# An attention and two-MoE kernel on one core: unused matmuls, the order of small transposes and differences in attention, and the place of a table load

## The chip, the cores and the metric

The kernel runs on one core of one Trainium2 chip. The metric is device microseconds (us) of one execution; lower is better. Three timed runs of the kernel before gave a median of 668.82 us (668.46 to 668.9). One further execution was profiled; all rows below are from it.

## The reference

Three stages in float32, each feeding the next:

```python
# attention: q, k, v are (2, 8, 576, 64); window 128; q and k are drawn 6.6 times larger than usual
scores = 0.125 * q @ k.T + bias                  # bias: -slope(head) * distance
scores = where((rel >= 0) & (rel < 128), scores, -1e9)
attn = exp(scores - max(scores)); attn = attn / (sum(attn) + 1e-9)
x = (attn @ v) reshaped to (1152, 512)
# MoE 1: four experts, w1 (4, 512, 1024), w2 (4, 1024, 512)
x = sum over e of p[:, e] * (relu(x @ w1[e]) @ w2[e])
# MoE 2: w_in (512, 2048), w_out (2048, 512), given as float64
h = x @ w_in
out = (h * cos(h)) @ w_out
```

## The kernel before, in words

Engines: TensorE (PE, its weight loads PEld), VectorE (DVE), ScalarE (ACT), GpSimd (POOL), and SyncE (SP), which issues the DMAs. The kernel switches the scheduler off, so each engine's queue holds its instructions in the order in which the loops write them.

**Attention** runs in 20 steps: two batches of five query blocks (the first of 64 rows, four of 128), each in two groups g = 0, 1 of four heads. `attention` (L494) is a software pipeline over k = 0 to 22. In round k, PE does the scores of step k (`att_scores`, L352, tile s_ps), the transposes of the probabilities of step k-2 (`att_transpose`, L419, tile t_ps; two halves m = 0 and m = 1) and the product with v of step k-3 (`att_pv`, L445, tile x_ps). DVE takes the row maxima of step k (L373), ACT the exponentials (L378); the half m = 0 of t_ps is copied out by DVE (L439), m = 1 by ACT (L441), both to tiles pt. There are two t_ps buffers, so a half of the next round can only be written when its copy of this round is done. For each query block (at g = 1) `att_sums` (L386, called one round after the scores) takes reciprocals of the row sums on DVE and spreads them on POOL (tile wide), and `att_factors` (L398, called two rounds after) transposes wide on PE (L405, tile r_ps), with a copy by ACT (L410, tile rs). `att_pv` then multiplies x_ps by rs on DVE (L469).

Between these calls stands `fill(k, s)`, s = 0, 1, 2 (L752), which spreads other work: for k < 9 at s = 0 two matmuls of the identity with itself whose result nobody reads (L757); the conversion of weights (`jobs`, on POOL); the first hidden layer of the first token block in halves (`plain`, L591, k = 12 to 19); three second-layer tiles (L666) at rounds 21 and 22; and `move`.

**The token blocks.** 1,152 tokens are three blocks of 384. The first goes through plain matmuls (operand xq). Blocks two and three go together through a product with seven multiplications in place of eight; its operands (tile xs) are made by `transform` (L282): three differences on DVE (t1, t2, b12; L299 to L301, shown at the helper's line L133), then seven roundings on ACT (L287) and seven remainders on DVE and POOL (L133), one `yield` after each. `transformed` (L327) runs the differences at once and leaves the rest in a list, from which `move(n)` (L335) takes n pieces. In attention it is called three times, in rounds 18, 20 and 22. The same function serves the turn from MoE 1 to MoE 2, there with a PSUM operand.

**The MoE groups** (`run`, L844) are 8 of MoE 1 and 4 of MoE 2, each a sequence of products (L569), plain matmuls (L597) and second layers (L666). Alongside, MoE 2's weights are converted from float64. In MoE 2 `cosine` (L533) evaluates cos as a Sin on ACT (L545); the activation table of that function is loaded by ACT_TABLE_LOAD, which in the kernel before stands directly ahead of the first such Sin.

Of the kernel before, what the change touches and what calls it, by code (L numbers as in the profile page):

```python
# [15 lines left out]
AF = mybir.ActivationFunctionType  # L16
# [18 lines left out]
NG1, NG2 = E * F1 // G, F2 // G  # L35
# [10 lines left out]
LAG = 2  # L46
# [3 lines left out]
def tile_kernel(ctx, tc, qT, kT, v, probs, w1, w2, w_in, w_out, out):  # L50
    nc = tc.nc
# [31 lines left out]
    def constants():  # L83
        rel_i, rel, msk = scr[:, 0].bitcast(I32), scr[:, 1], scr[:, 2]
        nc.gpsimd.iota(rel_i, pattern=[[-1, 256]], base=WIN, channel_multiplier=1)
        nc.vector.tensor_copy(rel, rel_i)
        nc.gpsimd.memset(msk, 0.0)
        big = -8.0e9
        nc.gpsimd.affine_select(
            out=msk, in_=msk, pattern=[[-1, 256]], compare_op=ALU.is_ge, fill=big,  # L90
            base=WIN, channel_multiplier=1,
        )
        nc.gpsimd.affine_select(
            out=msk, in_=msk, pattern=[[1, 256]], compare_op=ALU.is_ge, fill=big,
            base=-1, channel_multiplier=-1,
        )

        for h in range(H):
            slope = 2.0 ** (-8.0 * (h + 1) / H)
            nc.vector.scalar_tensor_tensor(  # L100
                out=bm[:, h, :], in0=rel, scalar=-8.0 * slope, in1=msk,
                op0=ALU.mult, op1=ALU.add,
            )
        make_identity(nc, ident)
# [18 lines left out]
    def load_values(b, i):  # L123
        s0, n = UNITS[i]
        vt = v_t[b, i] = qvp.tile([128, DM], F32, name="vt", tag="vt", bufs=5)
        nc.sync.dma_start(out=vt[:n], in_=v[b, s0 : s0 + n, :])
# [5 lines left out]
    def sub(eng, out, a, b):  # L132
        eng.tensor_tensor(out=out, in0=a, in1=b, op=ALU.subtract)  # L133
# [83 lines left out]
    def loads_ahead():  # L217

        if nload[0] < len(wq):
            raw_load(*wq[nload[0]])  # L220
            nload[0] += 1
# [60 lines left out]
    def transform(t, x1, x2, ps=None):  # L282

        def hi(k, src):
            nc.scalar.activation(out=xs[:, 0, k, :, ts], in_=src, func=AF.Copy)  # L287

        def lo(k, src, eng):
            sub(eng, xs[:, 1, k, :, ts], src, xs[:, 0, k, :, ts].bitcast(F32))  # L290

        ts = slice(t * 128, (t + 1) * 128)
        t1, t2 = (txp.tile([128, 2, 128], F32, name="tx", tag="tx") for _ in range(2))
        b11, b21, b12, b22 = x1[:, 0:2], x1[:, 2:4], x2[:, 0:2], x2[:, 2:4]
        if ps is None:
            ps = x2
        else:
            nc.scalar.activation(out=x2, in_=ps, func=AF.Copy)
        sub(nc.vector, t1, ps[:, 0:2], b11)  # L299
        sub(nc.vector, t2, ps[:, 2:4], t1)  # L300
        sub(nc.vector, b12, ps[:, 2:4], b12)  # L301
        yield

        hi(B11, b11)
        yield
        lo(B11, b11, nc.vector)
        hi(T2, t2)
        yield
        lo(T2, t2, nc.gpsimd)
        hi(T1, t1)  # L310
        yield
        lo(T1, t1, nc.vector)
        hi(T3, b12)
        yield
        lo(T3, b12, nc.gpsimd)
        hi(B21, b21)
        yield
        lo(B21, b21, nc.vector)
        sub(nc.vector, b21, b21, t2)
        hi(B22, b22)  # L320
        yield
        lo(B22, b22, nc.gpsimd)
        hi(T4, b21)
        yield
        lo(T4, b21, nc.vector)

    def transformed(*args):  # L327
        move(24)
        tr = transform(*args)
        next(tr)  # L330
        moved.append(tr)

    moved = []
# [1 line left out]
    def move(n):  # L335

        while moved and n:
            if next(moved[0], True):
                moved.pop(0)
            else:  # L340
                n -= 1
# [147 lines left out]
    def load_units_to(k):  # L489
        while nloaded[0] < min(k, len(units)):  # L490
            load_unit(*units[nloaded[0]])
            nloaded[0] += 1

    def attention(fill):  # L494
        at = lambda k, what: what(*steps[k]) if 0 <= k < len(steps) else None
        for k in range(len(steps) + LAG + 1):
            if k < len(steps) and k % 2 == 0:

                load_units_to(k // 2 + 3)
                load_values(*steps[k][0])  # L500
            at(k, att_scores)
            at(k - 1, att_sums)
            fill(k, 0)
            at(k - LAG, att_transpose)
            fill(k, 1)
            at(k - LAG - 1, att_pv)
            fill(k, 2)
            at(k - LAG, att_factors)


    pr = const.tile([128, NTT, E], F32, name="pr")
# [2 lines left out]
    def routing():  # L514
        nc.vector.tensor_reduce(out=prs, in_=pr, axis=mybir.AxisListType.X, op=ALU.add)
        nc.vector.tensor_scalar(out=prs, in0=prs, scalar1=1e-9, scalar2=None, op0=ALU.add)
        nc.vector.reciprocal(out=prs, in_=prs)
        nc.vector.tensor_tensor(
            out=pr, in0=pr, in1=prs.unsqueeze(2).to_broadcast([128, NTT, E]), op=ALU.mult
        )  # L520
# [6 lines left out]
    def advance():  # L527

        for ch in list(chains):
            if next(ch[1], True):  # L530
                chains.remove(ch)
# [59 lines left out]
    def plain(g, q, halves=False):  # L591

        w = operand(w_t[1, g, q // 2])
        ps = sums()[:, :NB]
        for d in range(ND):
            for a, bb in PASSES:
                nc.tensor.matmul(  # L597
                    ps, w(a, 2 * (q % 2) + d // 2, d % 2), xq[:, bb, d],
                    start=(d == 0 and (a, bb) == PASSES[0]),
                    stop=(d == ND - 1 and (a, bb) == PASSES[-1]),  # L600
                )
            if halves and d == 1:
                yield
        yield
        finish(g, ps, q, 0)
# [126 lines left out]
    def whole(step):  # L732
        for _ in step:
            pass

    with tc.manual_schedule():

        warm = ppool.tile([128, 4, 256], F32, name="warm", tag="p")
        nc.vector.memset(warm[:, 0], 0.0)
        nc.vector.memset(dens, 1e-9)  # L740
        for _ in range(WARM):
            nc.tensor.matmul(
                ps1.tile([128, 512], F32, name="o_ps", tag="o_ps")[:, :256],
                warm[:, 0, :128], warm[:, 0], start=True, stop=True,
            )
        load_units_to(2)
        constants()
        first = [None]

        turns = [(21, 1), (22, 1), (22, 2)]  # L750

        def fill(k, s):  # L752
            if s == 0 and k < 9:

                idle = ps1.tile([128, 512], F32, name="o_ps", tag="o_ps")
                for _ in range(2):
                    nc.tensor.matmul(idle[:, :128], ident, ident, start=True, stop=True)  # L757
            if (k, s) == (2, 0):
                for _ in range(RAWS):
                    loads_ahead()  # L760
            if (k, s) == (4, 0):
                nc.sync.dma_start(out=pr, in_=probs.rearrange("(t p) e -> p t e", p=128))
            if (k, s) == (11, 0):
                routing()
            if s == 0 and 4 <= k < 20:
                next(jobs)
            if s == 1 and 12 <= k < 20:
                q, half = divmod(k - 12, 2)
                if not half:
                    first[0] = plain(0, q, True)  # L770
                next(first[0])
            if s == 2 and 12 <= k < 20 and k % 2:
                whole(first[0])
            tile = None
            if (k, s) in turns:
                tile = layer2(0, turns.index((k, s)))
                next(tile)
            move(24 if (k, s) == turns[-1] else 2 * (s > 0))
            if tile:
                whole(tile)  # L780

        attention(fill)
    att.close()

# [59 lines left out]
    def run(groups):  # L844
        for g in groups:
            for step, stages, njobs, ncv in steps(g):
                next(step)
                move(2)
                for _ in range(stages):
                    advance()  # L850
                for _ in range(njobs):
                    next(jobs)
                for _ in range(ncv):
                    next(cv, None)
                next(step, None)
# [2 lines left out]
    cv = converts()  # L858
    with tc.manual_schedule():
        next(cv)  # L860
        run(range(NG1 - 1))
        left = sum(1 for _ in cv)
        assert not left, left
    cvs.close()
# [42 lines left out]
```

## Time and profile before

| | before |
|---|---|
| median of 3 runs | 668.82 us |
| the profiled execution | 669.17 us |
| its span, first to last instruction | 667.4 us |
| mean granted TensorE clock | 0.995 |
| PE busy | 654.1 us (98%) |
| DVE, ACT, POOL busy | 436.7, 331.5, 351.2 us |

The span is 1.77 us shorter than the time of the same execution, and that execution is 0.35 us above the median. Busy shares are averages over the span. A granted clock of 1.00 is TensorE at 2.4 GHz, 0.50 is 1.2 GHz.

### The profile page before, as it was taken

Reading aid. Unit: us, or ns where it says so; the run is one execution under the profiler, and the core shown is the slowest. Engines: PE = TensorE matmul, PEld = TensorE weight load, DVE = VectorE, ACT = ScalarE, POOL = GpSimd, SP = SyncE. Lnnn points to the kernel's source line nnn. Section 1 sums busy time; section 2 is a strip of 40 time slices with the busy share of each in tenths; the row PEclk is TensorE's granted clock in tenths of the full one; section 3 lists DMA queues with packets and bytes.
Section 4 is the critical chain, followed back from the end, with each engine's and each line's share of the span. In section 5 each row is a group of like instructions: output and inputs, shape, how many; then the busy total and the mean of one; then the engine's idle time right before and its main releaser. Section 6 shows DMA issues by size and latency. Waiting matters only on the chain.

```text
span 667.4 us, 9861 instructions
## 1 busy us (share of the span) xinstructions
PE 654.1 (98%) x3604; PEld 577.8 (87%) x3604; DVE 436.7 (65%) x830; ACT 331.5 (50%) x759; POOL 351.2 (53%) x342
## 2 busy tenths in 40 slices
PE   9999899999999999999999999999899999999998
PEld 7787689898998998998998988987798988988976
DVE  6675877868767768679678572546674563673662
ACT  6786635444343444353253341346673673673660
POOL 2664528447256265275174192284547747757740
PEclk9999899999999999999999999999899999999999
DMA  8362111624515426326326231120000200200102
GB/s 243 84 192 70 32 32 50 220 79 159 174 54 164 149 78 204 110 80 215 118 64 220 79 96 32 31 95 1 24 8 33 94 1 32 94 1 31 49 32 94
DMA packets 39872, 60.42 MB, mean 91 GB/s; under 512 B 5648, under 2 KB 22288, under 8 KB 39824
## 3 DMA queue, kind: packets, MB, share of 16 engines
q1 hardware_dynamic: 39824, 59.80, 28.2%
q8 instruction: 28, 0.46, 0.3%
q14 instruction: 20, 0.16, 0.1%
HBM read 49.04 MB, written 10.75 MB: 90 GB/s over the span
## 4 chain that ended last, share of the span: by engine, by line
PE 83%; DVE 8%; ACT 6%; issue 2%; POOL 1%; DVEq 0%; ACTq 0%; POOLq 0%
PE o_ps L666 38%; PE o_ps L569 21%; PE o_ps L597 13%; PE x_ps L457 3%; PE s_ps L362 3%; PE t_ps L429 2%; DVE u L541 2%; ACT r L539 2%; ACT u L538 2%; POOL hpair L133 1%; DVE u L547 1%; PE o_ps L757 1%; DVE c L612 1%; DVE xs L133 1%; DVE o_ps L612 1%
## 5 line engine op out<-in xcount | busy, mean ns | idle before, releaser
L666 PE MATMUL o_ps<-w2t,hpair 128*128 128x512 f32 x852 | 204.2, 392 | 1.6 <-POOL hpair L133 1.4
L666 PEld LDWEIGHTS o_ps<-w2t,hpair 128*128 128x128 f32 x852 | 158.6, 188 | 34.5 <-POOL hpair L133 2.7
L569 PE MATMUL o_ps<-xs,w1t 128*128 128x384 f32 x1008 | 183.0, 338 | 4.0 <-DVE c L612 3.1
L569 PEld LDWEIGHTS o_ps<-xs,w1t 128*128 128x128 f32 x1008 | 176.6, 189 | 8.5 <-DVE c L612 4.4
L597 PE MATMUL o_ps<-xq,w1t 128*128 128x384 f32 x576 | 110.4, 338 | 0.0
L133 POOL TENSOR_TENSOR w1t<-raw,w1t 128x512 fp32r<-128x512 f32 x48 | 65.1, 1367 | 84.3 <-ACT w1t L156 80.6
L133 POOL TENSOR_TENSOR w2t<-raw,w2t 128x512 fp32r<-128x512 f32 x48 | 67.3, 1419 | 70.9 <-ACT w2t L156 70.6
L597 PEld LDWEIGHTS o_ps<-xq,w1t 128*128 128x128 f32 x576 | 101.6, 188 | 3.3
L666 PE MATMUL o_ps<-w2t,h 128*128 128x512 f32 x432 | 103.7, 393 | 0.0
L666 PEld LDWEIGHTS o_ps<-w2t,h 128*128 128x128 f32 x432 | 81.0, 189 | 16.2 <-issue 0.2
L133 POOL TENSOR_TENSOR w1t<-sm,w1t 128x512 fp32r<-128x512 f32 x48 | 63.6, 1335 | 45.7 <-ACT w1t L156 45.4
L541 DVE SCALAR_TENSOR_TENSOR u<-r,u 128x384 f32<-128x384 f32 x48 | 39.9, 840 | 62.1 <-ACT r L539 58.5
L133 POOL TENSOR_TENSOR hpair<-u,hpair 128x384 fp32r<-128x384 f32 x32 | 33.0, 1054 | 39.5 <-ACT hpair L549 39.5
L156 ACT ACTIVATE w1t<-sm 128x512 fp32r<-128x512 f32 x44 | 27.5, 626 | 35.3 <-POOL sm L133 35.3
L378 ACT ACTIVATE p<-p,nmax 128x256 f32<-128x256 f32 (+2 forms) x80 | 36.2, 454 | 16.0 <-DVE nmax L373 15.8
L254 ACT ACTIVATE cr<-cr 128x512 f32<-128x512 f32 x32 | 21.6, 676 | 44.8 <-DVE cv L248 44.8
L681 DVE SCALAR_TENSOR_TENSOR accpair<-o_ps,pr,accpair 128x512 f32<-128x512 f32 x42 | 31.3, 745 | 17.8 <-PE o_ps L666 17.8
L556 ACT ACTIVATE hpair<-o_ps 128x384 fp32r<-128x384 f32 x48 | 23.4, 488 | 36.5 <-DVE o_ps L612 35.9
L242 ACT ACTIVATE cr<-cr 128x512 int32<-128x512 uint32 x32 | 21.6, 677 | 39.0 <-DMA cr<-w_in 27.0
L557 DVE SCALAR_TENSOR_TENSOR hpair<-o_ps,hpair 128x384 fp32r<-128x384 f32 x48 | 26.6, 554 | 20.3 <-ACT hpair L556 20.3
L248 DVE SCALAR_TENSOR_TENSOR cv<-cr,cv 128x512 int32<-128x512 int32 x32 | 34.1, 1066 | 1.1
L545 ACT ACTIVATE u<-u 128x384 f32<-128x384 f32 x48 | 24.7, 518 | 20.3 <-DVE u L541 20.3
(111 smaller groups left out, 833.7 us busy)
## 6 DMA issues: line engine op xcount, KB each, us to landing
raw<-w SPq DMA_DIRECT2D x32, 512.0 KB, 3.9
cr<-w_in SPq DMA_DIRECT2D x16, 512.0 KB, 4.4
cr<-w_out SPq DMA_DIRECT2D x16, 512.0 KB, 4.5
wi<-cv SPq DMA_DIRECT2D x16, 256.0 KB, 3.8
wo<-cv SPq DMA_DIRECT2D x16, 256.0 KB, 2.2
raw<-wi SPq DMA_DIRECT2D x8, 512.0 KB, 3.3
raw<-wo SPq DMA_DIRECT2D x8, 512.0 KB, 3.5
qt<-qT SPq DMA_DIRECT2D x8, 256.0 KB, 2.9
```

The source lines that it names most:

```text
L133: eng.tensor_tensor(out=out, in0=a, in1=b, op=ALU.subtract)
L156: nc.scalar.activation(out=out, in_=src, func=AF.Copy)
L248: nc.vector.scalar_tensor_tensor(out=a, in0=hw, scalar=-0x40000000, in1=o, op0=ALU.bitwise_and, op1=ALU.bitwise_or,)
L378: nc.scalar.activation(out=p[:n, k, :wid], in_=p[:n, k, :wid], func=AF.Exp, scale=-1.0, bias=nmax[:n, k : k + 1], accum_out=den[:n, k, 0:1],)
L541: nc.vector.scalar_tensor_tensor(out=u, in0=r, scalar=MAGIC, in1=u, op0=ALU.subtract, op1=ALU.subtract)
L545: nc.scalar.activation(out=u, in_=u, func=AF.Sin, scale=-TWOPI)
L556: nc.scalar.activation(out=hi, in_=src, func=AF.Relu)
L557: nc.vector.scalar_tensor_tensor(out=lo, in0=src, scalar=0.0, in1=hi.bitcast(F32), op0=ALU.max, op1=ALU.subtract)
L569: nc.tensor.matmul(ps, w(a, k, m), xs[:, bb, b, m], start=(start and m == 0 and (a, bb) == PASSES[0]), stop=(stop and m == 1 and (a, bb) = ...
L597: nc.tensor.matmul(ps, w(a, 2 * (q % 2) + d // 2, d % 2), xq[:, bb, d], start=(d == 0 and (a, bb) == PASSES[0]), stop=(d == ND - 1 and (a, ...
L666: nc.tensor.matmul(ps, h0[:, a, f, t * 128 : (t + 1) * 128] if t < NQ else hpair[:, a, f, (t - NQ) * 128 : (t - NQ + 1) * 128], w_t[2, g, ...
L681: nc.vector.scalar_tensor_tensor(out=o, in0=ps, scalar=s, in1=o, op0=ALU.mult, op1=ALU.add)
```

## The change

Four edits:

1. The two unused matmuls stand in rounds 0 to 3 only, no longer in rounds 4 to 8.
2. `att_factors` moves from the end of a round to directly behind `att_transpose`.
3. A `transform` that is called from attention starts with two empty pieces and is no longer advanced at once; `move` takes three pieces at s = 1, in place of two. So the differences of a block come one round later, behind that round's row maxima.
4. The table of Sin is loaded by an instruction of its own after group 0 of MoE 1.

```diff
@@ transform
         if ps is None:
+            yield
+            yield
             ps = x2
@@ transformed
         tr = transform(*args)
-        next(tr)
+        if len(args) > 3:
+            next(tr)
         moved.append(tr)
@@ attention
             fill(k, 0)
             at(k - LAG, att_transpose)
+            at(k - LAG, att_factors)
             fill(k, 1)
             at(k - LAG - 1, att_pv)
             fill(k, 2)
-            at(k - LAG, att_factors)
@@ fill
-            if s == 0 and k < 9:
+            if s == 0 and k < 4:
@@ fill
-            move(24 if (k, s) == turns[-1] else 2 * (s > 0))
+            move(24 if (k, s) == turns[-1] else (0, 3, 2)[s])
@@ the first MoE loop
         next(cv)
-        run(range(NG1 - 1))
+        run(range(1))
+        nc.scalar.preload_act_table(AF.Sin)
+        run(range(1, NG1 - 1))
```

PE in round 5, before: scores, the unused pair (o_ps from ident), transposes of the probabilities, product with v, transposes of wide.

```order
L362 MATMUL s_ps<-xk,qt 128x256 x4
L757 MATMUL o_ps<-ident 128x128 x2
L429 MATMUL t_ps<-ident,p 64x128 x2
L429 MATMUL t_ps<-ident,p 128x128 x2
L429 MATMUL t_ps<-ident,p 64x128 x2
L429 MATMUL t_ps<-ident,p 128x128 x2
L457 MATMUL x_ps<-pt,vt 64x128 x8
L405 MATMUL r_ps<-ident,wide 128x128 x4
```

The same round 5 after the change:

```order
L365 MATMUL s_ps<-xk,qt 128x256 x4
L432 MATMUL t_ps<-ident,p 64x128 x2
L432 MATMUL t_ps<-ident,p 128x128 x2
L432 MATMUL t_ps<-ident,p 64x128 x2
L432 MATMUL t_ps<-ident,p 128x128 x2
L408 MATMUL r_ps<-ident,wide 128x128 x4
L460 MATMUL x_ps<-pt,vt 64x128 x8
```

The unused pair is gone, and the four transposes of wide stand ahead of the product with v.

DVE at the end of round 18 and in round 19, the last with scores, before (L373's rows, ISA, are the row maxima; four pairs of them stand there; the tx and xk rows of L133 are the differences; xs is the first remainder):

```order
L439 COPY pt<-t_ps 128x512
L469 TENSOR_TENSOR xk<-x_ps,rs 128x512
L133 TENSOR_TENSOR tx<-xk 128x256
L133 TENSOR_TENSOR tx<-xk,tx 128x256
L133 TENSOR_TENSOR xk<-xk 128x256
L133 TENSOR_TENSOR xs<-xk,xs 128x2x128
L373 ISA p,nmax<-s_ps,bm 128x256
L373 ISA nmax 128x1
```

After the change, from the last pair of the row maxima on:

```order
L376 ISA p,nmax<-s_ps,bm 128x256
L376 ISA nmax 128x1
L442 COPY pt<-t_ps 128x512
L133 TENSOR_TENSOR tx<-xk 128x256
L133 TENSOR_TENSOR tx<-xk,tx 128x256
L133 TENSOR_TENSOR xk<-xk 128x256
L133 TENSOR_TENSOR xs<-xk,xs 128x2x128
L560 SCALAR_TENSOR_TENSOR h_128<-o_ps,h_128 128x384
L133 TENSOR_TENSOR xs<-tx,xs 128x2x128
L394 TENSOR_REDUCE rec<-dens 128x8
L397 RECIPROCAL rec<-rec 128x8
L442 COPY pt<-t_ps 128x512
```

The row maxima of step 19 and the copy of t_ps behind them now stand ahead of the differences; the copy of the next round stands behind the differences, three remainders and the reciprocal.

ACT at the turn to MoE 2, before (f_ps is a transposed output tile, u the argument of the cosine):

```order
L298 ACTIVATE accpair<-f_ps 128x512
L287 ACTIVATE xs<-accpair 128x2x128
L287 ACTIVATE xs<-tx 128x2x128
L545 ACT_TABLE_LOAD
L545 ACTIVATE u<-u 128x384
L156 ACTIVATE w1t<-sm 128x512
```

ACT where group 0 ends, after the change:

```order
L254 ACTIVATE cr<-cr 128x512
L559 ACTIVATE h_128<-o_ps 128x384
L865 ACT_TABLE_LOAD
L621 ACTIVATE p_1718<-o_ps 128x384
L156 ACTIVATE w2t<-raw 128x512 x2
```

The load has moved from the turn to the end of group 0; each program has two loads in all, the other being the one of Exp at the start.

## Rows read from the trace of the kernel before

**Rows 1.** The page, busy time by engine, and the granted clock in 40 slices.

```profile
PE 654.1 (98%) x3604; PEld 577.8 (87%) x3604; DVE 436.7 (65%) x830; ACT 331.5 (50%) x759; POOL 351.2 (53%) x342
...
PEclk9999899999999999999999999999899999999999
```

**Rows 2.** The chain of waits, 12 to 29 us: start, length, engine, tile, line.

```profile
12.79 0.64 PE o_ps L757 x4
...
14.68 1.06 PE s_ps L362 x8
...
28.62 0.64 PE o_ps L757 x4
```

**Rows 3.** The timelines of DVE and ACT: start, length, instruction; copies of t_ps in round 4.

```profile
14.53 0.70 DVE L439 COPY pt<-t_ps 64x256 f32<-64x256 f32 x2
...
15.34 0.63 ACT L441 ACTIVATE pt<-t_ps 64x256 f32<-64x256 f32 x2
```

**Rows 4.** Windows: length, then busy us of PE, PEld, DVE, ACT, POOL; clock, DMA, GB/s.

```profile
11.60:31.10 19.50, 19.50 (x186) 14.71 (x185) 12.20 (x55) 15.66 (x56) 11.04 (x13) 1.00 0.55 157
31.10:40.20 9.10, 9.10 (x106) 7.27 (x104) 6.92 (x36) 8.32 (x33) 7.84 (x11) 1.00 0.60 171
```

**Rows 5.** The second of these windows, the transposes of L429 alone: PE, PEld.

```profile
31.10:40.20 9.10, 3.28 (x24) 2.57 (x24) 1.00 0.60 171
```

**Rows 6.** The timeline of PE in rounds 19 and 20; in brackets idle time and releaser.

```profile
68.73 1.14 PE L362 MATMUL s_ps<-kt,qt 64*128 64x256 f32 x8
...
72.89 0.66 PE L405 MATMUL r_ps<-ident,wide 128*128 128x128 f32 x4
75.53 0.66 PE L429 MATMUL t_ps<-ident,p 128*128 128x128 f32 x4 [1.98 <-DVE pt L439]
```

**Rows 7.** The chain of waits, 60 to 92 us.

```profile
69.64 0.82 DVE tx L133
...
73.50 0.33 DVE p L373
...
75.95 0.48 ACT pt L441
...
78.03 0.48 ACT rs L410
...
79.05 1.95 PE t_ps L429 x8
```

**Rows 8.** The timeline of DVE, the first difference of the next block.

```profile
80.77 0.43 DVE L133 TENSOR_TENSOR tx<-xk 128x256 f32<-128x256 f32 x1
```

**Rows 9.** Windows around the two slices with a lower clock.

```profile
75.00:80.00 5.00, 3.87 (x29) 3.07 (x30) 3.38 (x9) 4.61 (x14) 1.49 (x3) 0.74 0.13 49
80.00:85.00 5.00, 5.00 (x36) 4.04 (x35) 4.50 (x10) 2.13 (x6) 2.89 (x4) 0.92 0.01 3
460.00:465.00 5.00, 4.04 (x21) 3.09 (x20) 4.32 (x8) 2.63 (x6) 1.82 (x3) 1.00 0.02 3
480.00:485.00 5.00, 5.00 (x19) 4.65 (x18) 2.70 (x6) 3.69 (x8) 2.65 (x3) 0.66 0.35 107
```

**Rows 10.** The chain of waits at the turn to MoE 2.

```profile
453.33 1.28 ACT L545
...
454.62 0.53 ACT u L545
...
479.48 3.65 PE o_ps L569 x12
```

**Rows 11.** The timeline of DVE there: the operation on whose result the first Sin works.

```profile
453.44 0.55 DVE L541 SCALAR_TENSOR_TENSOR u<-r,u 128x384 f32<-128x384 f32 x1
```

**Rows 12.** PE's waits from 450 to 490 us: total, times, longest.

```profile
PE o_ps L569 <- DVE c L612: 2.1, 1, 2.1
PE f_ps L714 <- DVE accpair L681: 1.0, 1, 1.0
```

**Rows 13.** The timeline of ACT at the end of group 0.

```profile
132.66 0.49 ACT L618 ACTIVATE p<-o_ps 128x384 f32<-128x384 f32 x1 [1.11 <-PE o_ps L569]
```

## The prediction

> **What bounds the kernel now.** I read the page first. PE is busy 98% of the span [rows 1], so a gain must take work from PE, fill one of its few idle stretches, or raise its clock. The line of the granted clock shows two of 40 slices below 9: the fifth, 67 to 83 us, the end of attention, and the 29th, 467 to 484 us, the turn to MoE 2 [rows 1, 9]. The chain of waits then says who sets the pace. From 5 to 68 us it is PE without a break, with the unused pairs in it (five of them from 12 to 29 us [rows 2]). From 69 to 79 us it leaves PE for DVE and ACT [rows 7], and again up to 479.5 us at the turn, with the table load as one link [rows 10]. Apart from the first microsecond PE waits nowhere else for longer than 0.7 us. All four edits touch these places.
>
> **Edit 1, the unused pairs.** Rounds 4 to 8 each lose 0.64 us of PE on the chain: 5 x 0.64 = 3.2 us [rows 2]. Between 11.6 and 31.1 us PE is never idle [rows 4], so these are real time, unless what PE would meet 0.64 us earlier isn't ready. ACT is the next limit: it works 15.66 us in that window, PE would need 19.5 - 3.2 = 16.3, so ACT is close behind but not ahead [rows 4]. Round by round I find one wait. In round 5 the scores would end at 15.1 (12.79, plus 1.25 for the transposes and the product with v of round 4, plus 1.06 for the scores). The transposes behind them need both copies of t_ps of round 4. DVE's ends at 14.53 + 0.70 = 15.2, ACT's at 15.34 + 0.63 = 16.0 [rows 2, 3]. The second half, due near 15.6, waits about 0.4 us. Later rounds have their copies 0.5 us or more before the need, because there ACT's work moves up along with the scores. What is saved is 3.2 - 0.4 = **2.8 us**. The bounds are 3.2 (no wait) and 0 (ACT takes over in every round). I stay near the first, since rounds 9 to 11 run without pairs already and PE does not idle there, with ACT busy 8.32 of 9.10 us [rows 4].
>
> What else could the pairs be for? The clock. In rounds 9 to 11 there is no pair and no hidden layer, transposes of t_ps fill 3.28 of the 9.10 us, and the clock is 1.00 throughout [rows 4, 5]. So I price the loss of the pairs' cover at nothing. The Trainium skill speaks against this edit: in "TensorE: Matmul & The Clock Gate", Part 4, it says that the clock's upper level does not engage for transposes, which do not count as PE activity in the same way. By that rule the rounds without pairs could fall to the lower level; that is a rival below, priced from rows.
>
> **Edit 2, the factors' transposes.** The same four matmuls, 0.66 us [rows 6], come about 1 to 2 us earlier in the round. They need wide, which POOL finishes in the round before, so PE does not wait. ACT then finds r_ps ready right behind its copy of t_ps. PE is the bound in these rounds, so by itself this is **0**; it only helps edit 3. Its cost bound is a wait for wide, a few tenths.
>
> **Edit 3, the differences.** Before, step 15's product ends and DVE starts on the differences at 69.64; the row maxima of the last scores, ready at 68.73 + 1.14 = 69.87, start only at 73.50 [rows 6, 7]. Everything behind them is late by 3.6 us: DVE's copy of t_ps, for which PE waits 1.98 us [rows 6], then ACT's exponentials and copies, for which it waits twice more for 0.3. And the clock: 0.74 over 75 to 80 us and 0.92 over 80 to 85 means (0.26 x 5 + 0.08 x 5) x 2 = 3.4 us at 1.2 GHz [rows 9], in which work takes twice as long. That costs 1.7 us; the eight transposes at 79.05 take 1.95 in it [rows 7], 1.0 at the upper level. As one sum: PE ends the factors' transposes at 73.5 [rows 6] and starts the last block of transposes at 79.05, 5.6 us for transposes and a product that take about 1.0 each at the upper level: 3.6 lost. With 0.9 more for the slow transposes, 4.5 us are lost.
>
> After: the row maxima start at 69.9. From their start to ACT's copy of t_ps it is 75.95 - 73.50 = 2.45 us [rows 7], so the copy runs from 72.35 to 72.8. DVE's copy, right behind the row maxima (four at 0.35), ends near 71.9. PE comes to the transposes of round 20 at 73.5, as before [rows 6], and finds both: **the wait of 1.98 is gone**. PE then does transposes and product until 75.6. Late next is the copy of round 20 on DVE, now behind more work. From 72.35 ACT does its copy (0.48 [rows 7]), rs (as much), two roundings, the hidden layer's rounding and a third rounding, an estimated 2.3 us, to 74.7; DVE then that rounding's remainder (0.4, as the operation of [rows 8]), the reciprocal (an estimated 0.3) and the copy (0.7 [rows 3]), to 76.1 or, with a pause or two, 76.4. So PE waits 0.5 to 0.9 us; I take 0.9. The differences themselves cost less there: 0.43 each when POOL is quiet, against 0.82 [rows 7, 8]. A wait of this size leaves the clock up: from 460 to 465 us PE is idle for 0.96 and the clock stays 1.00 [rows 9, 12]. So the edit saves 4.5 - 0.9 = **3.6 us**. Bounds: 4.5 (no wait left) and 0 (the wait comes back whole one round later). The last block's differences were the last thing before the products of MoE 1; one remainder now stands ahead of them on DVE, 0.4 us, where PE had about as much to spare, so nothing for that.
>
> **Edit 4, the table load.** It takes 1.28 us at 453.33; the first Sin starts at 454.62 [rows 10]. Its argument is ready at 453.44 + 0.55 = 453.99 [rows 11]. Without the load Sin could start at 454.0, so **0.6 us** leave a chain that runs through DVE and ACT from there to 479.48 without PE [rows 10]. PE collects them in its wait of 1.0 us on the accumulator, which shrinks to 0.4 [rows 12]; the wait of 2.1 behind it stays, since both sides move. Bounds 0 and 1.28. At its new place the load fills ACT's pause of 1.11 us [rows 13] and makes ACT 0.2 late; the product's copy is needed by a second pass of PE more than 2 us on. Cost 0. No table load is added after it, since all that ACT does from there on (copy, relu, abs, Sin) stands behind one load in the built order.
>
> **Sum.** 2.8 + 0 + 3.6 + 0.6 = 7.0 us. Against the profiled execution, 669.17, that is 662.2; that execution lies 0.35 above the median, so I predict **661.8 us**. Between 92 and 450 us PE waits for nothing, so what is gained in attention is handed on. A measurement of this kernel can tell some 0.2%, 1.3 us, from no change.
>
> **Rivals.**
> - *The wait moves.* PE finds round 20's copy on DVE later than I reckon, idles some 2 us and the clock falls as before; edit 3 then gives about 1.0 in place of 3.6: 664.4. For it: eleven DVE operations with waits on ACT stand ahead of that copy. Against: each is priced from rows, and POOL is quieter by then.
> - *ACT takes over.* The pairs were hidden; edit 1 gives 0.3 in place of 2.8: 664.3. For it: ACT at 15.66 of 16.3. Against: rounds 9 to 11 [rows 4].
> - *Better: the second slow stretch goes too.* At 480 to 485 the clock is 0.66, again 3.4 us at 1.2 GHz and 1.7 us lost, after PE's wait of 2.1 [rows 9, 12]. That wait now falls at another moment of the run. If the clock then stays up: 661.8 - 1.7 = 660.1.
> - *Slower: the clock falls in attention.* Without pairs, rounds 4 to 8 run at 1.2 GHz. Their 16.3 us of PE work [rows 4] take 16.3 more: 678.1. It decides once about 14 us are spent at the lower level, since each costs half and the gain is 7.0. For it stands only the skill's sentence above; against it, the clock of 1.00 in rounds 9 to 11 [rows 4, 5].
> - *No change.* The edits don't do what they say. The built order shows that they do; what is left is that the wait moves and ACT takes over at once, and the load was hidden: within 0.2%, 668.
>
> **Chances.** Forecast 0.52; the wait moves 0.20; ACT takes over 0.09; better 0.12; slower 0.04; no change 0.03. The first four are faster: 0.93. The range goes from the better case to just beyond the two weaker gains, 659.7 to 664.9; it leaves out the last two cases and some of the mixed ones (wait moved and pairs hidden, 666.9).
>
> **What would show it.** Right: the slice at the end of attention has clock 9; no wait of PE on L439's copy of about 2 us, but one under 1 us at the last block of transposes; the scores of round 9 start 2.8 us earlier; the first product of MoE 1 starts 6.4 us earlier; PE's wait on the accumulator at the turn is near 0.4. Wrong: a wait of PE in each of rounds 4 to 8; a slow slice between 12 and 40 us; a PE wait of 2 us or more in rounds 20 or 21; a pause of PE near 131 us; or a third ACT_TABLE_LOAD.

## The result, and the profile after

The changed kernel takes **661.44 us** (median of 5 executions, 661.05 to 661.97), the kernel before, on the same chip, 668.82 (668.32 to 669.02, 5 executions). The ratio is 0.9892, with a 95% interval of 0.9877 to 0.9906: faster by 1.1%. The prediction was 661.8 with a range of 659.7 to 664.9. The execution that was profiled took 661.97, its span is 660.2 and its mean granted clock 0.999. Line numbers are 2 or 3 higher than before: L362 is now L365, L429 is L432, L405 is L408, L439 and L441 are L442 and L444, L569 is L572.

The page after, busy time by engine and the granted clock, beside [rows 1]:

```profile
PE 649.2 (98%) x3584; PEld 573.0 (87%) x3584; DVE 435.2 (66%) x830; ACT 330.7 (50%) x759; POOL 350.8 (53%) x342
...
PEclk9999999999999999999999999999999999999999
```

PE has 20 matmuls fewer, the five pairs (each matmul of a pair is two instructions here), and 4.9 us less of busy time. Both slices with a lower clock are gone.

The waits of PE over the whole span: total, times, longest.

```profile
PE o_ps L572 <- DVE c L615: 3.0, 4, 2.1
...
PE o_ps L572 <- ACT p L621: 1.1, 3, 0.6
...
PE f_ps L717 <- DVE accpair L684: 0.3, 1, 0.3
```

No line on pt is left, where before PE waited 1.98 us on DVE's copy [rows 6]. The wait on the accumulator fell from 1.0 to 0.3, and the one on c is as long as it was [rows 12]. New is 0.6 us on ACT, at 482.51.

The chain of waits in rounds 4 to 9:

```profile
12.36 1.11 PE s_ps L365 x8
...
16.06 0.54 ACT pt L444 x2
...
16.64 0.63 PE t_ps L432 x4
17.27 0.44 PE r_ps L408 x4
...
22.73 1.06 PE s_ps L365 x8
23.80 1.02 PE t_ps L432 x8
...
29.39 1.06 PE s_ps L365 x8
```

The same chain before, with a pair up to round 8 and none from round 9 on:

```profile
11.81 0.98 PE s_ps L362 x8
...
25.07 0.87 PE t_ps L429 x8
...
31.16 1.06 PE s_ps L362 x8
32.23 1.02 PE t_ps L429 x8
```

The transposes now come directly behind the scores. From the scores of round 4 to those of round 9 it is 29.39 - 12.36 = 17.03 us, against 31.16 - 11.81 = 19.35 before: 2.32 less. Only once in these rounds does the chain leave PE, between the scores of round 4 and the transposes of round 5, for the exponentials of round 4 and ACT's copy behind them (16.06). Without a wait the transposes of round 5 would end at 16.88 (its scores end at 15.86, plus 1.02); they end at 17.27, so 0.4 us are lost. Two things were not forecast: eight transposes take 1.02 us here where they took 0.87 behind a pair, and the factors' transposes take 0.44 where they took 0.59. Round 4 itself starts 0.55 later than in the profile of before. That is start-up: the first pair takes 1.15 us here and 0.73 there, the scores behind it 0.59 and 0.38, together 0.63, and the factors' transposes of round 3 give 0.08 back. Up to there the two kernels have the same order on PE but for these; the first pair takes 0.64 to 1.15 us in the profiles of this case.

The timeline of PE in rounds 19 to 21:

```profile
67.44 1.09 PE L432 MATMUL t_ps<-ident,p 128*128 128x128 f32 x8
...
70.98 1.09 PE L432 MATMUL t_ps<-ident,p 128*128 128x128 f32 x8
...
73.19 1.36 PE L432 MATMUL t_ps<-ident,p 128*128 128x128 f32 x8
```

The timeline of DVE there, the last row maximum and what now stands behind it:

```profile
68.58 0.42 DVE L376 CUSTOM_DVE_ANT_0 p<-s_ps,bm 128x256 f32<-128x256 f32 x1
...
68.92 0.69 DVE L442 COPY pt<-t_ps 128x512 f32<-128x512 f32 x1
69.53 0.50 DVE L133 TENSOR_TENSOR tx<-xk 128x256 f32<-128x256 f32 x1
```

The end of the chain in attention:

```profile
66.44 1.11 PE s_ps L365 x8
67.56 0.41 DVE p L376
...
73.28 0.57 DVE pt L442
...
73.89 0.66 PE t_ps L432 x4
74.54 0.44 PE r_ps L408 x4
...
85.66 9.40 PE o_ps L572 x53
```

The same before; at 68.83 the product ends and the scores of round 19 begin:

```profile
67.78 1.05 PE x_ps L457 x16
...
92.09 14.59 PE o_ps L569 x84
```

The transposes of round 20 (70.98) follow without a break. At the last block (73.19) PE idles 0.17 us before the first half and a little between the halves, 0.5 in all (the product ends at 72.00 + 1.02 = 73.02 and the transposes would end at 74.04; they end at 74.54). From the scores of round 19 to the first product of MoE 1 it is 85.66 - 66.44 = 19.22 us, before 92.09 - 68.83 = 23.26: 4.04 less.

So the first product of MoE 1 starts 6.43 us earlier (92.09 to 85.66): 2.32 from rounds 4 to 8, 0.62 from rounds 9 to 18, 4.04 from the end of attention, less 0.55 of start-up. In that product 0.18 is lost again (its 84 matmuls take 14.77 us, 14.59 before; a weight load waits 0.2 for DVE's c).

The timeline of ACT at the new place of the load:

```profile
125.32 1.28 ACT L865 ACT_TABLE_LOAD   x1
126.62 0.49 ACT L621 ACTIVATE p<-o_ps 128x384 f32<-128x384 f32 x1
```

At the turn PE comes to the accumulator 6.25 us earlier than before and leaves it 6.86 earlier (462.59 to 455.73): the load is worth 0.61.

The product behind the wait on c, in the timeline of PE, where before it took 3.65 us [rows 10]:

```profile
472.62 2.35 PE L572 MATMUL o_ps<-xs,w1t 128*128 128x384 f32 x12 [2.06 <-DVE c L615]
```

### The profile page after: what moved, and what is told of

Same layout as the page of the kernel before. It is cut to its first block, busy times and chain, and to the rows that moved or that the text cites. A ratio compares the mean times of both kernels' runs of the same rounds, so it can differ in the third digit from the quotient of the medians.

```text
span 660.2 us, 9818 instructions
## 1 busy us (share of the span) xinstructions
PE 649.2 (98%) x3584; PEld 573.0 (87%) x3584; DVE 435.2 (66%) x830; ACT 330.7 (50%) x759; POOL 350.8 (53%) x342
## 4 chain that ended last, share of the span: by engine, by line
PE 83%; DVE 7%; ACT 6%; issue 2%; POOL 1%; ACTq 0%; DVEq 0%; POOLq 0%
PE o_ps L669 38%; PE o_ps L572 21%; PE o_ps L600 14%; PE s_ps L365 3%; PE x_ps L460 3%; DVE u L544 2%; PE t_ps L432 2%; ACT r L542 2%; ACT u L541 2%; POOL hpair L133 1%; DVE u L550 1%; DVE c L615 1%; DVE xs L133 1%; DVE o_ps L615 1%; ACT p L381 1%
## 5 line engine op out<-in xcount | busy, mean ns | idle before, releaser
L572 PE MATMUL o_ps<-xs,w1t 128*128 128x384 f32 x1008 | 182.5, 336 | 4.8 <-DVE c L615 3.0
L572 PEld LDWEIGHTS o_ps<-xs,w1t 128*128 128x128 f32 x1008 | 175.5, 188 | 10.2 <-DVE c L615 4.8
L133 POOL TENSOR_TENSOR w1t<-raw,w1t 128x512 fp32r<-128x512 f32 x48 | 65.0, 1364 | 84.3 <-ACT w1t L156 80.7
L133 POOL TENSOR_TENSOR w2t<-raw,w2t 128x512 fp32r<-128x512 f32 x48 | 67.2, 1418 | 71.2 <-ACT w2t L156 70.9
L133 POOL TENSOR_TENSOR w1t<-sm,w1t 128x512 fp32r<-128x512 f32 x48 | 63.4, 1330 | 45.0 <-ACT w1t L156 44.7
L133 POOL TENSOR_TENSOR hpair<-u,hpair 128x384 fp32r<-128x384 f32 x32 | 32.6, 1039 | 39.5 <-ACT hpair L552 39.5
```

The costliest lines, as they stand in the source:

```text
L572: nc.tensor.matmul(ps, w(a, k, m), xs[:, bb, b, m], start=(start and m == 0 and (a, bb) == PASSES[0]), stop=(stop and m == 1 and (a, bb) = ...
```

## The experiments

Eleven kernels in twelve runs: each edit alone, two edits left out of the whole, and variants of the pairs and of the two orders. Each expectation stands as it was written before the run. "Before" is the kernel before on the same chip. The interval of a ratio, in brackets, is some 0.9 us to either side (0.6 for edits 2 and 4 alone), so times alone tell two variants apart only from about 1.3 us on; smaller differences between variants rest on the traces.

**Edit 1 alone** (the kernel before with this):

```diff
-            if s == 0 and k < 9:
+            if s == 0 and k < 4:
```

> Edit 1 alone: the unused pairs in rounds 0 to 3 only. Theory P (the prediction's term): 5 x 0.64 = 3.2 us less 0.4 of one wait, 2.8 us gained, near 666.0. Theory S (from the two traces): the transposes behind the scores take 1.02 us on the chain, behind a pair 0.87, so a pair costs PE only 0.49 net; 5 x 0.49 = 2.4, less 0.5 of waiting in round 5: 1.9 gained, near 666.9. Rival (the pairs hold the clock up): a granted clock of 0.5 somewhere between 12 and 40 us, and no gain or a loss.

666.45 us (665.81 to 667.48, 5 executions), before 668.78; ratio 0.9968 (0.9956 to 0.9981): 2.3 us. The chain of waits of its profile, rounds 4 to 9:

```profile
12.40 1.04 PE s_ps L362 x8
...
18.70 0.59 PE r_ps L405 x4
...
23.91 1.02 PE t_ps L429 x8
...
29.66 1.06 PE s_ps L362 x8
```

29.66 - 12.40 = 17.26, so 2.09 less than before. The time lies between the two theories, 2.8 and 1.9, and its interval (1.3 to 2.9 us) holds both; the trace decides for Theory S. The transposes take 1.02 here too, so the 0.15 us that they lose belong to the missing pair, while r_ps keeps its 0.59.

**Edit 2 alone:**

```diff
             at(k - LAG, att_transpose)
+            at(k - LAG, att_factors)
...
-            at(k - LAG, att_factors)
```

> Edit 2 alone: the factors' transposes directly behind the probabilities' ones. Theory P: 0, PE does the same work, 668.8. Theory S: behind transposes of the same shape the four take 0.44 us on the chain in place of 0.59 behind the product with v, in eight rounds with 128 rows and two with 64 (0.08 less): 8 x 0.15 + 2 x 0.08 = 1.4 at most, less the one or two rounds in which PE waits anyway; near 667.6.

667.79 us (667.38 to 669.18, 11 executions), ratio 0.9986 (0.9977 to 0.9995): 1.0 us where I had 0. The profile of this run is also the test of the clock's share, since its granted clock is 9 in every slice of its page and 1.00 in the mean. Its timeline of PE at the end of attention:

```profile
74.61 0.66 PE L429 MATMUL t_ps<-ident,p 128*128 128x128 f32 x4 [2.14 <-DVE pt L439]
...
78.12 0.66 PE L429 MATMUL t_ps<-ident,p 128*128 128x128 f32 x4 [0.88 <-ACT pt L441]
79.28 0.66 PE L429 MATMUL t_ps<-ident,p 128*128 128x128 f32 x4 [0.51 <-DVE pt L439]
```

Its first difference, in the timeline of DVE:

```profile
68.64 0.88 DVE L133 TENSOR_TENSOR tx<-xk 128x256 f32<-128x256 f32 x1
```

Its window over the same stretch as in [rows 9]:

```profile
75.00:80.00 5.00, 3.32 (x34) 2.44 (x33) 3.36 (x9) 3.79 (x11) 1.93 (x3) 1.00 0.00 0
```

At the upper level the last block's transposes still start at 78.12 and 79.28, because they wait for ACT and DVE (0.88 and 0.51). From the first difference (68.64 here, 69.64 before [rows 7]) to the end of these transposes it is 11.30 us here (79.28 + 0.66) and 11.36 before (79.05 + 1.95). The slow stretch cost no time: it filled a wait. The executions of the kernel before say the same. Of 21 in this comparison, 12 have a mean granted clock of 0.995, with a median of 668.70, and 7 have 1.00, with 668.85.

**Edit 3 alone:**

```diff
         if ps is None:
+            yield
+            yield
...
-        next(tr)
+        if len(args) > 3:
+            next(tr)
...
-            move(24 if (k, s) == turns[-1] else 2 * (s > 0))
+            move(24 if (k, s) == turns[-1] else (0, 3, 2)[s])
```

> Edit 3 alone: the differences behind the next round's row maxima. Theory P: 3.6 us gained, 665.2; PE's wait of 2 us on the copy of t_ps gone, the slow stretch at the end of attention gone. Rival (the gain needs edit 2, because ACT's copy of r_ps then comes late in the round and the remainders behind it): a wait of over 1 us stays at the last block of transposes, the gain is 2.5 or less.

665.09 us (664.74 to 665.24, 5 executions), ratio 0.9945 (0.9931 to 0.9958): 3.7 us, as forecast. The list of PE's waits has none on a copy of t_ps any more (at the last block 0.17 us are left on the chain, behind ACT's copy). The first product of MoE 1 starts at 87.60, against 92.09; rounds 4 to 9 take 19.35, as before. From the scores of round 19 to that product it is 87.60 - 68.47 = 19.13 us, against 23.26: in the trace the edit gives 4.1.

**Edit 4 alone:**

```diff
-        run(range(NG1 - 1))
+        run(range(1))
+        nc.scalar.preload_act_table(AF.Sin)
+        run(range(1, NG1 - 1))
```

> Edit 4 alone: the table of Sin loaded after group 0. Theory P: 0.6 us gained, 668.2: PE's wait of 1.0 us on the accumulator at the turn shrinks to 0.4, and nothing is added near 131 us. Rival 1 (the load was hidden, another link takes its place): 0, the wait stays at 1.0. Rival 2 (the load is not free at its new place): a wait of PE near 131 us.

667.93 us (667.55 to 668.63, 11 executions), ratio 0.9988 (0.998 to 0.9997): 0.9 us. The wait on the accumulator is 0.3, and no wait appears near the load's new place. The four edits alone add up to 2.3 + 1.0 + 3.7 + 0.9 = 7.9 us, together they give 7.4: within the noise they do not overlap.

**No pairs at all** (the changed kernel with this):

```diff
-            if s == 0 and k < 4:
+            if s == 0 and k < 0:
```

> The changed kernel without any unused pair, also none in rounds 0 to 3. Theory L: ACT works without a pause through rounds 0 to 4 (its exponentials stand back to back from 5.9 to 12.5 us before the change), so PE only gets to its next wait sooner: 0 to 0.6 us gained against the changed kernel, 660.9 to 661.4. Rival 1: PE is the bound there too, 4 x 0.49 = 2.0 gained, 659.5. Rival 2 (the pairs hold the clock up): a granted clock of 0.5 between 5 and 20 us, slower than the changed kernel.

661.91 us (661.1 to 663.93, 5 executions), ratio 0.9909 (0.9896 to 0.9923): no gain over the change, and a wider spread. Three lie at 661.1 to 661.9, two at 663.6 and 663.9. The profile fell on the shortest.

**The same once more, for a profile of a long execution:**

> The kernel without any pairs once more, for one profile. Of its five timed runs two were some 2.3 us longer than the others, and the profile fell on a short one. If this profile falls on a long one, Theory K wants a stretch below 1.00 in the granted clock before 30 us, and PE's scores of round 9 some 2 us later than in the first profile; Theory H wants the clock at 1.00 there, and the 2 us elsewhere. On a short one it tells nothing new: 661 to 662.

663.99 us: a long one. Its chain of waits:

```profile
6.19 2.37 PE s_ps L365 x13
...
12.52 2.01 PE s_ps L365 x8
14.53 1.84 PE t_ps L432 x8
...
18.25 0.99 PE t_ps L432 x8
...
21.15 1.06 PE s_ps L365 x8
```

The chain of the first profile without pairs, 661.10 us:

```profile
11.53 1.11 PE s_ps L365 x8
...
18.35 1.06 PE s_ps L365 x8
```

Weight loads of the same eight transposes, in the long one:

```profile
14.46 1.51 PEld L432 LDWEIGHTS t_ps<-ident,p 128*64 128x64 f32 x8 [0.65 <-issue]
```

and in the short one:

```profile
12.53 0.82 PEld L432 LDWEIGHTS t_ps<-ident,p 128*64 128x64 f32 x8 [0.33 <-issue]
```

The window of the long one in that stretch:

```profile
14.00:17.00 3.00, 3.00 (x22) 1.98 (x18) 2.36 (x12) 1.91 (x8) 0.59 (x2) 1.00 1.01 302
```

From 6 to 17 us work on PE takes about 1.8 times as long: scores 2.01 against 1.11, transposes 1.84 against 0.99 a round later, their weight loads 1.51 against 0.82. By the scores of round 6 it is 21.15 - 18.35 = 2.80 us late, which is the whole difference of the two executions (2.89). The DMA share, 1.01, is no higher than in the short one (1.09), and 1.84 is about what the transposes took in the slow stretch before (1.95 [rows 7]). This looks like the lower clock level, but the row of the granted clock reads 1.00 there, so Theory K has its 2.8 us before round 6, but not the clock below 1.00 that it wanted in the row. The Trainium skill has a caution for this: in "TensorE: Matmul & The Clock Gate", Part 1, Seeing it yourself, it says that the clock's trace events on trn2 have been observed to be unreliable. These rows would fit it, with 1.84 us of transposes under a row that reads 1.00; that the clock was low is not shown.

**Pairs in rounds 0 and 1 only:**

```diff
-            if s == 0 and k < 4:
+            if s == 0 and k < 2:
```

> The changed kernel with the unused pairs in rounds 0 and 1 only (before: 0 to 8, the change: 0 to 3). Theory H (a pair costs its 0.45 to 0.49 us wherever PE sets the pace, and nothing where PE waits): rounds 2 and 3 are near the start, where the run without any pairs showed new waits of the scores on DVE (0.8 us) and gained nothing in the time; so at most 0.9 us are gained, 660.5 to 661.4, with a spread like that of the change (under 1 us). Theory K (the pairs of the first rounds hold the clock): some runs come out some 2 us longer than others, as two of the five without any pairs did, and in a profile the granted clock lies below 1.00 somewhere before 20 us; median 661.4 or more, spread over 2 us.

661.58 us (661.48 to 662.02, 4 executions), ratio 0.9895 (0.9881 to 0.991): the change's time and no wide spread. The spread is Theory H's, but the gain of up to 0.9 that it allowed did not come; Theory K's spread over 2 us and clock below 1.00 did not come either (the profiled execution has 1.00). So pairs in rounds 0 and 1 do all that pairs in rounds 0 to 3 do.

That they keep PE from the slow start is likely but not shown. For it: three of six executions without pairs were long, none of the nine with pairs in two or four rounds; and in all twelve profiles with pairs at the start the second pair is back at 0.64 us from 7.4 us on at the latest, while one of the two profiles without is slow up to 17. Against taking it as shown: the numbers are small, and kernels with pairs spread by up to 1.8 us too (edit 2 alone, 667.38 to 669.18). Why PE starts slow in one execution and not in another is open.

**Pairs in rounds 4 to 8, but behind the transposes** (the changed kernel with this):

```diff
-            if s == 0 and k < 4:
+            if (s == 0 and k < 4) or (s == 1 and 4 <= k < 9):
```

> The changed kernel with the unused pairs of rounds 4 to 8 put back, but behind the transposes, not behind the scores. Theory S (a pair behind the scores takes over 0.15 us that the transposes else lose there): here a pair costs its whole 0.64, the transposes keep 1.02, so up to 5 x 0.64 = 3.2 slower than the changed kernel, near 664.4. Theory P (a pair costs 0.64 anywhere and was offset by waits): as edit 1 alone in reverse, 2.1 to 2.3 slower, 663.6 or less.

663.5 us (663.07 to 663.76, 4 executions), ratio 0.9918 (0.9905 to 0.9932): 2.1 more than the change. The time is Theory P's and the transposes' 1.02 is Theory S's; the price of the pair is neither's. Its chain of waits:

```profile
18.95 1.06 PE s_ps L365 x8
20.01 1.03 PE t_ps L432 x8
21.04 0.45 PE o_ps L760 x4
```

A pair takes 0.45 us here and 0.64 behind the scores [rows 2], and the transposes behind the scores take 1.03, against 0.87. Whoever comes first behind the scores pays 0.15 to 0.19 us more. So taking the pair away gives 0.64 - 0.15, about 0.49, in each round; put back here, five pairs cost 5 x 0.45 = 2.25, less the 0.4 of round 5's wait that they fill: 1.85, and rounds 4 to 9 of this trace are 1.83 longer than in the change.

**Factors ahead of the probabilities' transposes:**

```diff
-            at(k - LAG, att_transpose)
             at(k - LAG, att_factors)
+            at(k - LAG, att_transpose)
```

> The changed kernel with the factors' transposes ahead of the probabilities' ones, directly behind the scores. Theory X (PE loses some 0.15 us where the shape of its work changes, whoever comes first): the four transposes of wide now take 0.59 again, and the probabilities' ones behind them 0.87 where they take 1.02 in the changed kernel; the sum of a round is unchanged and the time is that of the change, 661.4 within 0.5. Theory Y (the 0.15 us belong to the factors' transposes and the product with v ahead of them): they take 0.44 here, and the probabilities' ones stay at 1.02. Either way the copies of the probabilities' transposes come 0.5 us later, which may cost up to 0.5 at the end of attention.

662.43 us (661.66 to 662.82, 4 executions), ratio 0.9909 (0.9892 to 0.9925). Its chain of waits, a round with factors:

```profile
21.42 1.06 PE s_ps L365 x8
22.48 0.59 PE r_ps L408 x4
23.07 0.87 PE t_ps L432 x8
```

Its list of PE's waits has a new line:

```profile
PE r_ps L408 <- POOL wide L399: 1.0, 1, 1.0
```

Theory X: r_ps takes 0.59 again, now that it comes first, and the transposes behind it are back at 0.87; the sum is 1.46, as in the change (1.02 + 0.44). The time is 1.0 longer, about the noise between two variants. In the trace 0.62 of it lie at the end of attention, where PE waits 1.0 us for POOL's wide, which is late for its new place (85.33 - 65.49 = 19.84 us from the scores of round 19 to the first product, 19.22 in the change). My expectation had looked for up to 0.5 there, and on the copies.

**Everything but edit 2:**

```diff
-            at(k - LAG, att_factors)
...
+            at(k - LAG, att_factors)
```

> The changed kernel without edit 2 (edits 1, 3 and 4). Theory S (the factors' transposes take 0.15 us less each time behind transposes): 0.9 to 1.3 us slower than the changed kernel, 662.3 to 662.7, with 0.59 per four transposes on the chain again. Theory P: no difference, 661.4. Rival (edit 3 needs edit 2): more than 1.5 slower, with a wait of PE at the last transposes of over 0.5.

662.89 us (661.83 to 663.0, 4 executions), ratio 0.9906 (0.9893 to 0.992): edit 2 is worth 1.45 in company by the medians and 0.9 by the two ratios. Eight blocks of 128 rows at 0.59 - 0.44 = 0.15 and two of 64 at 0.33 - 0.25 = 0.08 would be 1.36, but the trace has less. From the scores of round 4 to those of round 19 it takes 67.31 - 12.45 = 54.86 us against 54.08 in the change, 0.78 more; from there to the first product it takes 19.10 against 19.22, so in the last rounds, where PE has to wait for DVE and ACT, the edit gives nothing. It isn't there to help edit 3: without it no wait on a copy of t_ps is listed either.

**Everything but edit 3:**

```diff
-            move(24 if (k, s) == turns[-1] else (0, 3, 2)[s])
+            move(24 if (k, s) == turns[-1] else 2 * (s > 0))
```

(with `transform` and `transformed` as before)

> The changed kernel without edit 3 (edits 1, 2 and 4). Theory D (the time lost at the end of attention is that of DVE's and ACT's chain, whatever the clock does): 3.7 us slower, 665.1, and runs with and without the slow stretch at the end of attention take the same time within 0.4. Theory C (of the loss, 1.7 is the clock's): runs with the slow stretch are 1.7 longer than runs without it.

665.32 us (664.63 to 665.77, 5 executions), ratio 0.9945 (0.9933 to 0.9958): edit 3 is worth 3.9 in company by the medians; in the trace it is 89.30 - 65.98 = 23.32 us from the scores of round 19 to the first product, 19.22 in the change, so 4.1. The wait on DVE's copy is back at 2.1. The executions at a mean clock of 0.995 took 665.32, 664.63 and 664.81, those at 1.00 took 665.77 and 665.69: once more the slow stretches cost nothing.

**Differences one place later**, behind the multiplication of the product with v:

```diff
-            move(24 if (k, s) == turns[-1] else (0, 3, 2)[s])
+            move(24 if (k, s) == turns[-1] else (0, 2, 2)[s])
```

> The changed kernel with two pieces at s = 1 in place of three, so that the differences stand behind the multiplication of the product with v on DVE, at s = 2, and one piece fewer is done by the end. Theory D (what counts is that the row maxima stand ahead of the differences): nothing is lost at round 19, and the 0.17 us that PE still waits at round 20 can go: 661.2 to 661.6. Theory L (the pieces that come later are missing at the end): the products of MoE 1 wait for the last operands, some 0.5 to 1.5 us: 662 to 663.

662.96 us (662.61 to 663.32, 4 executions), ratio 0.9915 (0.99 to 0.993): 1.5 more than the change. The waits of PE in its profile:

```profile
PE o_ps L572 <- DVE xs L133: 1.4, 2, 1.0
```

The first product of MoE 1 now waits 1.0 us for its operands, as Theory L said. The three pieces at s = 1 are part of what the edit is worth. No variant beat the change.

## Why the prediction was right

The mechanism of three of the four edits held, the terms were mis-sized in opposite directions, and one reason was wrong without harm. That the sum, 7.0 against 7.4, came closer than its terms is in part luck: edit 1 was some 0.7 too high, edits 2 and 3 together 1 or more too low.

- **Edit 1, predicted 2.8, measured 2.1 to 2.3.** The one wait that I found, in round 5, is there, at the 0.4 predicted. What the step missed is that a pair costs 0.64 on the chain but takes over 0.15 of the transposes' time behind it: 5 x 0.49 is 2.45, not 3.2, and with the wait 2.05. That rounds 9 to 11 run without pairs already, which the prediction used for ACT and the clock, could have shown it, since transposes took 1.02 there and 0.87 in rounds with a pair.
- **Edit 2, predicted 0, measured 1.0 alone and 0.8 to 1.45 in company.** The step that failed is that the same four matmuls come earlier at the same price, 0.66 us: they take 0.15 less behind transposes than behind the product with v. That the edit only helps edit 3 failed too: edit 3 loses nothing without it.
- **Edit 3, predicted 3.6, measured 3.7 alone and 3.9 in company, 4.1 in the traces of both.** The row maxima start at 67.56, right behind their scores, and the wait of 1.98 is gone. The wait left is 0.5 in all, where I took 0.9 from a bound of 0.5 to 0.9. The reason that failed is the clock's: 1.7 of the 4.5 us lost were put down to work at 1.2 GHz, and the run of edit 2 alone loses as much at 1.00 (11.30 us against 11.36). The sum survived because it was also taken as PE's whole delay between two points, which is the delay of the chain through DVE and ACT.
- **Edit 4, predicted 0.6, measured 0.61 in the trace**, 0.9 (0.2 to 1.3) alone in time. The load at its new place made nobody wait.
- **The point on the chain**: the first product of MoE 1 starts 6.43 us earlier, 6.4 predicted; but 0.55 of late start-up in that profile hides that attention gave about 7.0.
- **The rivals.** The wait did not move and ACT did not take over. The better case, the second slow stretch gone, happened in the profile and brought nothing near 1.7: the product at 472.62 took 2.35 us at the upper level, where 3.65 were needed before [rows 10], but PE then waited 0.59 for ACT and was only 0.47 further ahead behind it (at 485.98, before 493.31, so 7.33 after 6.86). Nor does the time depend on it: three of the change's five executions have a mean clock of 0.997 and took 661.05 to 661.44, the two at 0.999 and 1.00 took 661.97 and 661.58. Two variants profiled at 0.997 (factors ahead, differences one place later) have the low clock at the turn, 0.79 over 470 to 478 us, so the stretch is not gone in every execution. The slower case did not come in rounds 4 to 8: the clock reads 1.00 and the transposes keep 1.02. The sentence of the Trainium skill ("TensorE: Matmul & The Clock Gate", Part 4), that the clock's upper level does not engage for transposes, is not borne out in these rounds, where scores and products stand between the transposes. If pairs matter anywhere it is in the first rounds, which the change leaves alone.

## What to carry to other kernels

Read what an instruction costs from rows with the same instruction ahead of it: filler that is removed also hid something, here a quarter of its own time. A stretch at a lower clock is a loss only if the engine ends the waits there; if another chain sets the time, the clock turns a wait into slow work and back. Before removing filler, ask in which rounds it could keep the engine going: here it was useless in rounds 4 to 8 and, as far as fifteen executions tell, useful in the first two.

## What was not expected of the hardware

TensorE took some 0.15 us more for the same work behind the scores or the product with v than behind transposes or a pair. Eight transposes take 1.02 us behind scores and 0.87 behind a pair or behind wide's transposes; the four of wide take 0.59 behind scores or the product with v and 0.44 behind the other transposes; a pair takes 0.64 behind scores and 0.45 behind transposes. In the rows of these rounds the scores work as 64*128 and the product with v as 128*64, the others as 128*128, so the loss goes with a change of that form; other changes of form were not compared, and what in the engine costs it was not separated. Grouping transposes that go to different tiles therefore saved time without removing anything.

Near the start PE can work at about half its rate while the row of the granted clock reads 1.00, in one execution without pairs from 6 to 17 us; it shows only in the durations. Two executions of that one kernel differ by 2.8 us for it. In the profile of the change the first pair takes 1.15 us, where later ones take 0.64, which looks like a short form of the same; its cause is open too.
